# Stage A of sequences 4 to 7 as four 64x64 matmuls in the quadrants of the array

## The chip, the cores and the metric

The kernel runs on one core of one Trainium2 chip. The metric is the device time of one execution in microseconds (us), as the median of several runs. Each core has a matrix engine (PE, with its weight loads listed apart as PEld), a vector engine (DVE), a scalar engine (ACT), a general engine (POOL, which also issues DMAs) and a queue engine (SP, which issues most DMAs).

## The reference

Each of 8 sequences of 3008 rows and 256 channels is filtered in the frequency domain, and a gated feed-forward layer follows on the 24064 rows.

```python
X = np.fft.rfft(x, axis=1)                       # x: (8, 3008, 256)
Y = X * (filt_r + 1j * filt_i)[None, :, :]
y = np.fft.irfft(Y, n=3008, axis=1).reshape(24064, 256)
xn = y / np.sqrt(np.mean(y * y, axis=-1, keepdims=True) + 1e-06) * rms_g
g = xn @ w_gate                                  # d_ff = 1536
out = (g / (1 + np.exp(-g)) * (xn @ w_val)) @ w_out
```

## The kernel before

**The transform.** 3008 = 64 x 47, so the row index of a sequence is split into n2 (64 values) and n1 (47 values, padded to 48). Stage A transforms over n2 with one matmul for two n1 columns of 256 channels. Since n2 has 64 values and the array 128 rows, the x tile holds n1 = i in one half of its partitions and n1 = 24 + i in the other; the weights `wa` are block-diagonal, so that half of the 128x128 array multiplies zeros. In the kernel before the two halves alternate from partition to partition. Four x tiles of 6 n1 pairs make a sequence, and stage A has 12 units (`a_unit`, L201), each one matmul of 512 columns, and one copy out of PSUM by ACT or DVE. The result goes to DRAM (`z_store`, L209, a 384 KB DMA per x tile on SP's queue) and comes back with another axis on the partitions (`t2_load`, L219). Stage B (`b_unit`, L236) transforms over n1 and multiplies with the filter (`s_part`, L223, on DVE); its table is `wb`. The inverse stages follow (`bi_unit`, L280, `n_unit`, L306), then the norm on POOL, and transposes by DMA.

**The feed-forward layer.** 48 blocks (`b`, `m`) of up to 512 rows times 12 column groups `jt` make 576 items. An item is `gv` (L533: two matmuls for the gate, two for the value, 512 columns each, then a silu on ACT and a product on DVE) and, two items later, `down` (L554: four matmuls of 256 columns). The loop over the items, at the end of the kernel, is the frame into which all else is laid: the work of sequence b is put between the items of the sequences before it.

**The order.** It is written out by hand, and each engine works through its instructions in that order. A planner (`at`, `fit`, `a_plan`, `b_plan`, `norm_plan`) gives every unit an item as its slot; `fit` moves a unit later until its PSUM bank ("M" for pool psM, "B" for pool psB, each one bank) is free in that slot and ACT's and DVE's planned backlog stays under a bound. In `a_plan` (L764) the units of sequences 4 to 7 are asked for at slots `t - 87 + 4 * i`, where t is the first item of sequence b - 1; after each third unit a `z_store` follows one slot later, and the `x_load` (L174) of the same tile of the next sequence two slots later at the earliest. x tiles have 4 buffers, stage A's results (`t1`) have 3.

**The head.** Before the first item, sequence 0 is transformed in an order of its own (`a0_unit`, `f_unit`, `b_unit`, `yt0_unit` and others), while POOL issues the loads of x, the filter (`f_load`), the tables and the weights (`w_load`, L590) and writes negated filter columns (`f_neg`, L407) that `s_part` with e = 1 reads. Here too lie the only matmuls of the kernel whose operands are a few partitions high: the small transposes on L650 and L651, of one and two partitions, between matmuls on the full array.

**Names that the steps below touch.** `psa`: stage A's PSUM tile; `xc`: x tile; `pf`: output of the filler matmuls that `fill` (L423) issues in the head; `hh`, `po`: input and output of `down`; `pg`, `pv`: outputs of `gv`; `ws`, `fs`: staging tiles of weights and filter; `ff`: the filter as `s_part` reads it.

Of the kernel before, what the change touches and what calls it, by code (L numbers as in the profile page):

```python
# [17 lines left out]
N1 = 47  # L18
# [20 lines left out]
def _make_tables():  # L39
    n2 = np.arange(N2)  # L40
    wa = np.zeros((P, P))
    wai = np.zeros((P, P))
    for h in range(2):
        r = slice(h, P, 2)
        for k2 in range(K2):
            c = np.cos(2 * np.pi * ((n2 * k2) % N2) / N2)
            s = np.sin(2 * np.pi * ((n2 * k2) % N2) / N2)
            re = 4 * k2 + 2 * h
            wa[r, re] = c
            wai[re, r] = c * (1.0 if k2 == 0 else 2.0)  # L50
            if k2 == 0:
                alt = 1.0 - 2.0 * (n2 % 2)
                wa[r, re + 1] = alt
                wai[re + 1, r] = alt
            else:
                wa[r, re + 1] = -s
                wai[re + 1, r] = -2.0 * s
    n1 = np.arange(N1)
    rows = (n1 // H) * 2 * H + n1 % H
    re, im = rows, rows + H  # L60
    wb = np.zeros((P, K2, KR))
    wi0 = np.zeros((KR, KR))
    for k2 in range(K2):
        for q in range(SL):
            if q < H:
                k = k2 + 64 * q
                sign = 1.0
            else:
                j = q - H + 1
                k = 64 * j - (k2 if k2 else 32)  # L70
                sign = -1.0
                if j == H and k2:
                    continue
            th = 2 * np.pi * ((n1 * k) % N) / N
            c, sn = np.cos(th), np.sin(th)
            if k == 0 or k == NF - 1:
                sn = np.zeros(N1)
            if k2:
                wb[re, k2, q] = c
                wb[im, k2, q] = sign * sn  # L80
                wb[re, k2, SL + q] = -sn
                wb[im, k2, SL + q] = sign * c
            else:
                part = re if q < H else im
                wb[part, k2, q] = c
                wb[part, k2, SL + q] = -sn
                m = 1.0 if k in (0, NF - 1) else 2.0
                wi0[q, part] = m * c
                wi0[SL + q, part] = -m * sn
    f = np.float16  # L90
    r = np.arange(KR)
    wi = np.zeros((P, K2, KR))
    wi[:KR] = wb[:KR].transpose(2, 1, 0)
    wi[:KR, 0, :] = wi0
    wi[:, :, (r % H) * NR + r // H] = wi * S_INV_B
    tab = np.concatenate([wa.astype(f), (wai * S_INV_A).astype(f), np.eye(P).astype(f),
                          np.eye(P).astype(np.float32).view(f)], axis=1)
    return tab, wb.astype(f), wi.astype(f)


@with_exitstack
def kernel(
# [10 lines left out]
):  # L113
    nc = tc.nc

    tab_np, wb_np, wi_np = _make_tables()
    tab_d = nc.inline_tensor(tab_np, name="tab_t").ap()
    wb_d = nc.inline_tensor(wb_np, name="wb_t").ap()
    wi_d = nc.inline_tensor(wi_np, name="wi_t").ap()

    z_d = nc.dram_tensor("z_tmp", (B, K2, KR, D), FP16, kind="Internal").ap()

# [22 lines left out]
    idf = tab[:, 3 * P:5 * P].bitcast(FP32)  # L145
    wb = glob.tile([P, K2, KR], FP16)
    wi = glob.tile([P, K2, KR], FP16)
    uu = glob.tile([P, H, 2, P], FP16)
    left = glob.tile([P, 2, K2, 2], FP16)
    va = uu.rearrange("p c e t -> p (c e t)").rearrange("p (e k j) -> p e k j", e=2, k=K2)  # L150
# [16 lines left out]
    def raw(src, row, ap):  # L167
        return bass.AP(tensor=src.tensor, offset=src.offset + row * D, ap=ap)
# [5 lines left out]
    def x_load(b, c):  # L174
        t = xp.tile([P, XC, D], FP16, tag="xc", name="xc")
        row = b * N + c * XC
        src = lambda n, w, lo=0: raw(x.flatten_outer_dims(), row + lo, [[N1 * D, n], [H * D, 2], [1, w * D]])
        if b == B - 1 and c == NXC - 1:
            w = XC - 1
            nc.vector.memset(t[96:P, w, :], 0.0)  # L180
            nc.gpsimd.dma_start(t[:, 0:w, :].rearrange("p a d -> p (a d)"), src(N2, w))
            nc.gpsimd.dma_start(t[0:P - 2, w, :], src(N2 - 1, 1, w))
            nc.gpsimd.dma_start(t[P - 2:P - 1, w, :],
                                raw(x.flatten_outer_dims(), row + w + (N2 - 1) * N1, [[D, 1], [1, D]]))
        else:
            nc.gpsimd.dma_start(t.rearrange("p a d -> p (a d)"), src(N2, XC))  # L186
        st[b]["x"][c] = t
# [5 lines left out]
    def copy(eng, out, in_, scale=None):  # L193
# [4 lines left out]
        else:  # L198
            nc.vector.tensor_scalar(out=out, in0=in_, scalar1=scale, scalar2=None, op0=ALU.mult)

    def a_unit(b, i, eng="A", bk=0):  # L201
        c, r = divmod(i, XC // 2)
        if r == 0:
            st[b]["t1"][c] = t1p.tile([P, XC, D], FP16, tag="t1", name="t1")
        ps = bank(bk, "psa")
        nc.tensor.matmul(ps, wa, st[b]["x"][c][:, 2 * r:2 * r + 2, :], start=True, stop=True)  # L206
        copy(eng, st[b]["t1"][c][:, 2 * r:2 * r + 2, :], ps.rearrange("p (a d) -> p a d", a=2))

    def z_store(b, c):  # L209
        dst = z_d[b].rearrange("k (m i) d -> k m i d", m=NR)[:, :, c * XC:(c + 1) * XC, :]  # L210
        nc.sync.dma_start(dst, st[b]["t1"][c])

    def t2_tile(b, c):
        if b == 0 and c == 3:
# [65 lines left out]
    def bi_unit(b, i, eng="A", bk=0, ks=slice(0, 4)):  # L280
        g, dh = divmod(i, 2)
        yt = st[b]["yt"][g]
        ps = bank(bk, "psi")[:, 0:4 * KR].rearrange("p (k j) -> p k j", k=4)
        for k in range(4)[ks]:
            nc.tensor.matmul(ps[:, k, :], yt[0:KR, k, dh, :], wi[0:KR, 4 * g + k, :], start=True, stop=True)  # L285
        dst = uu[:, :, dh, 16 * g:16 * g + 16].rearrange("p c (k m) -> p c k m", k=4)
        copy(eng, dst[:, :, ks], ps.rearrange("p k (c m) -> p c k m", c=H)[:, :, ks])
        done[b] += ks.stop == 4
        if done[b] == K2 // 2:
            half = uu[:, H - 1, :, :].rearrange("p e (k m) -> p e k m", k=K2)  # L290
            if b % 2:
                nc.gpsimd.tensor_copy(out=half[:, :, :, 2:4], in_=left)
            else:
                nc.gpsimd.tensor_copy(out=left, in_=half[:, :, :, 0:2])

    def t4_load(b, c):
        t = t4p.tile([P, XC, D], FP16, tag="t4", name="t4")
# [312 lines left out]
    with tc.manual_schedule():  # L610
# [14 lines left out]
        nc.gpsimd.dma_start(wb[:, 16:K2, :], wb_d[:, 16:K2, :])  # L625
        nc.gpsimd.dma_start(wb[:, 0:4, :], wb_d[:, 0:4, :])
        nc.gpsimd.dma_start(wi, wi_d)
        w_load(0)
        w_load(1)
        nc.vector.memset(mhalf, -0.5)  # L630
# [133 lines left out]
        def a_plan(b, slots):  # L764
# [11 lines left out]
                        at(max(s + 2, XAT.get(b + 1, (0,) * 4)[i // 3]), x_load, b + 1, i // 3)  # L776
            return s + 1

        def b_plan(b, slots, lags, soft=()):
            for c in range(4):  # L780
                at(slots[0] - 4 + c if c < 3 else slots[4] + 1, t2_load, b, c)
            for i in range(16):
                if i in soft:
                    s0 = fit(slots[i], ("B", 0, 1), ("A", 0, 0.5))
                    at(s0, b_soft, b, i)
                else:
                    opts = [(k, ((k, 0, 1), (k, 1, 1), ("V", 0, 0.55), ("V", 1, 0.55)))
                            for k in ("BM" if b == 1 else "B")]
                    k, need = min(opts, key=lambda o: fit(slots[i], *o[1], keep=False))
                    s0 = fit(slots[i], *need)  # L790
                    at(s0, b_unit, b, i, 0 if k == "M" else 3)
                    at(s0 + 1, s_part, b, i, 1)
                    at(s0 + 2, add_unit, b, i)
                if i % 2:
                    at(s0 + 3 + (i in soft), yt_load, b, i // 2)
                    for u in (i - 1, i):
                        last = fit(s0 + lags[u % 2], ("M", 0, 1), ("A", 0, 0.49))
                        at(last, bi_unit, b, u)
            return last
# [10 lines left out]
        for b in range(1, B):  # L810
            t = (b - 1) * 72
            if b == 1:
                z = a_plan(b, [i for i in range(12)])
                b_at, lags = [z + 7 + 7 * i // 5 for i in range(16)], (9, 9)
                soft = range(2, 16, 4)
            elif b == 2:
                z = a_plan(b, [28 + 3 * i for i in range(12)])
                b_at, lags, soft = [z + 13 + 7 * i // 3 for i in range(16)], (8, 9), ()
            else:
                at_ = [72 + 3 * i if b == 3 else t - 87 + 4 * i for i in range(12)]  # L820
                z = a_plan(b, [s - (s % JT == 1) for s in at_])
                b_at, lags, soft = [t - (25 if b == 3 else 26) + 4 * i for i in range(16)], (8, 12), ()
            assert z + 3 <= b_at[0] - 4
            end = b_plan(b, b_at, lags, soft)
# [5 lines left out]
                norm_plan(b, m, (n_at + 8 * m, n_at + 8 * m + (4 if b > 1 else 2)), (2, 3, 7) if b > 1 else (2, 3, 6))  # L830

        for i, now in plan.items():
            if any(fn == a_unit and a[3] == 0 for fn, a in plan.get(i + 1, ())) and bi_unit in [fn for fn, _ in now]:
                now.sort(key=lambda u: u[0] == sq_unit)

        stores = {}
# [48 lines left out]
```

## Time and profile before

| what | value |
|---|---|
| median of 3 runs | 863.04 us (862.97 to 863.13) |
| span of the profiled execution | 861.4 us |
| PE busy in the span | 852.4 us (99%) |
| DVE, ACT, POOL busy | 557.2, 612.4, 297.8 us |
| TensorE clock granted, all 40 slices | 9 tenths or more |
| DMA, mean over the span | 125 GB/s |
| stage A matmuls on L206 | 84, from 38.5 to 605.1 us |
| of these, in sequences 4 to 7 | 48, from 234 to 612 us |

The span is the time from the first to the last instruction of the program in one execution under the hardware profiler; what the timed run has beyond it, 863.04 - 861.4 = 1.6 us, lies around it. In the lists of instructions a matmul's own duration includes the way through the array, so that consecutive ones overlap: the time from the start of one to the start of the next says what it costs. PEld rows are weight loads, which run beside the matmul before.

### The profile page before, as it was taken

The numbers are of one execution on the slowest core, as the hardware profiler recorded it, in microseconds if no ns is written. First come the engines' busy times: TensorE is split into PE (matmuls) and PEld (weight loads), VectorE is DVE, ScalarE is ACT, GpSimd is POOL, SyncE is SP. The second block draws the span as 40 slices with busy tenths as digits, with TensorE's granted clock in tenths as the row PEclk, the third lists the DMA queues.
The fourth block names the chain that finished last, engine by engine and source line by source line (L and its number), as shares of the span: only waits on it lengthen the run. The fifth ranks groups of instructions, "written<-read, shape, count | busy, mean of one in ns | idle before, by whom it ended". The sixth has DMA issues, their size and how long they took to land.

```text
span 861.4 us, 17024 instructions
## 1 busy us (share of the span) xinstructions
PE 852.4 (99%) x6142; PEld 532.2 (62%) x6142; DVE 557.2 (65%) x926; ACT 612.4 (71%) x1339; POOL 297.8 (35%) x346
## 2 busy tenths in 40 slices
PE   8999999999999999999999999999999999999997
PEld 6755666566666666666666666666666666665664
DVE  5857655776666666666666676767666665555554
ACT  4986777787588756887577856888567765777443
POOL 5725742453144322534034430444123430132000
PEclk9999999999999999999999999999999999999999
DMA  9995778765975476656755548433564331521101
GB/s 283 270 204 124 150 164 168 139 130 121 197 137 129 121 150 111 151 107 147 139 127 113 132 98 180 108 87 101 131 127 93 97 70 42 124 54 49 62 25 50
DMA packets 198237, 107.98 MB, mean 125 GB/s; under 512 B 158566, under 2 KB 182520, under 8 KB 198152
## 3 DMA queue, kind: packets, MB, share of 16 engines
q1 hardware_dynamic: 189464, 85.52, 44.1%
q0 software_dynamic: 8544, 21.24, 12.7%
q8 instruction: 48, 0.79, 0.4%
q14 instruction: 37, 0.30, 0.1%
q10 hardware_dynamic: 144, 0.13, 0.0%
HBM read 45.78 MB, written 35.65 MB: 95 GB/s over the span
## 4 chain that ended last, share of the span: by engine, by line
PE 96%; DMA 1%; ACT 1%; DVE 1%; issue 0%; POOL 0%; POOLq 0%
PE po L563 28%; PE pg L546 28%; PE pv L546 28%; PE psb L241 3%; PE psi L285 3%; PE psn L314 2%; PE psa L206 2%; DMA fs<-in_filt_i_dram 1%; PE psy L418 1%; PE psf L389 1%; PE pst L367 0%; ACT sg L550 0%; POOL xc L186 0%; DVE s L231 0%; DVE hh L551 0%
## 5 line engine op out<-in xcount | busy, mean ns | idle before, releaser
L551 DVE TENSOR_TENSOR hh<-pv,sg 128x512 f16<-128x512 f32 (+2 forms) x578 | 391.5, 678 | 286.4 <-ACT sg L550 221.9
L550 ACT ACTIVATE sg<-pg 128x512 f16<-128x512 f32 (+2 forms) x578 | 337.4, 584 | 217.6 <-PE pg L546 213.4
L546 PE MATMUL pg<-xn,wg 128*128 128x512 f16 (+2 forms) x1156 | 338.1, 374 | 0.1
L546 PE MATMUL pv<-xn,wv 128*128 128x512 f16 (+2 forms) x1156 | 338.1, 374 | 0.0
L563 PE MATMUL po<-wo,hh 128*128 128x256 f16 x2256 | 332.7, 273 | 0.0
L563 PEld LDWEIGHTS <-hh 128*128 128x128 f16 x2256 | 213.4, 98 | 105.5 <-issue 0.6
L268 POOL TENSOR_TENSOR ss<-s,s 128x384 f16<-128x384 f16 x112 | 101.9, 911 | 273.2 <-DVE s L234 245.2
L546 PEld LDWEIGHTS <-wv 128*128 128x128 f16 x1156 | 112.9, 98 | 130.7
L546 PEld LDWEIGHTS <-wg 128*128 128x128 f16 x1156 | 111.4, 98 | 17.0 <-issue 0.3
L340 POOL TENSOR_TENSOR xt<-y,rho 128x1024 f16<-128x1024 f32 (+1 forms) x46 | 85.4, 1856 | 2.8
L322 ACT ACTIVATE junk<-y 128x256 f16<-128x256 f32 x180 | 74.3, 413 | 2.8
L231 DVE TENSOR_TENSOR s<-psb,ff 128x384 f16<-128x384 f32 x124 | 67.6, 547 | 0.7 <-ACT ff L195 0.6
L234 DVE TENSOR_TENSOR s<-psb,ff 128x384 f16<-128x384 f32 x124 | 67.6, 546 | 0.0
L195 ACT ACTIVATE uu<-psi 128x384 f16<-128x384 f32 (+1 forms) x127 | 61.6, 486 | 1.5 <-DMA out_dram<-o 0.5
L195 ACT ACTIVATE y<-psn 128x512 f32<-128x512 f32 (+1 forms) x95 | 55.7, 588 | 4.2
L285 PEld LDWEIGHTS <-yt 96*128 96x128 f16 x512 | 35.4, 97 | 26.7 <-issue 1.0
L332 POOL TENSOR_TENSOR rho<-u,mhalf 128x4 f32<-128x4 f32 (+1 forms) x46 | 46.5, 1010 | 3.8
L330 POOL TENSOR_SCALAR u<-ss 128x4 f32<-128x4 f32 (+1 forms) x46 | 8.9, 193 | 104.8 <-ACT junk L322 103.8
L195 ACT ACTIVATE t<-psa 128x512 f16<-128x512 f32 x70 | 41.4, 594 | 3.1 <-PE psa L206 1.7
L285 PE MATMUL psi<-wi,yt 96*128 96x96 f16 x512 | 42.9, 205 | 0.1
L241 PE MATMUL psb<-wb,t 96*128 96x96 f16 x480 | 40.1, 206 | 0.3 <-DVE s L234 0.2
L241 PEld LDWEIGHTS <-t 96*128 96x128 f16 x480 | 28.7, 97 | 12.8 <-DVE s L234 3.3
(101 smaller groups left out, 366.2 us busy)
## 6 DMA issues: line engine op xcount, KB each, us to landing
out_dram<-o SPq DMA_DIRECT2D x40, 512.0 KB, 3.6
xc<-in_x_dram POOLq DMA_DIRECT2D x31, 384.0 KB, 5.6
z_tmp<-t SPq DMA_DIRECT2D x28, 384.0 KB, 2.7
t<-z_tmp SPq DMA_DIRECT2D x28, 384.0 KB, 6.0
out_dram<-o SPq DMA_DIRECT2D x7, 384.0 KB, 2.7
fs<-in_filt_i_dram POOLq DMA_DIRECT2D x3, 512.0 KB, 10.8
fs<-in_filt_r_dram POOLq DMA_DIRECT2D x3, 512.0 KB, 11.2
ws<-in_moe_w_gate_dram POOLq DMA_DIRECT2D x3, 512.0 KB, 9.8
```

The lines of the kernel that those rows point to most:

```text
L195: nc.scalar.activation(out=out, in_=in_, func=AXT.Copy, **({} if scale is None else {"scale": scale}))
L231: eng.tensor_tensor(out=o, in0=ps, in1=f1, op=ALU.mult)
L234: eng.tensor_tensor(out=o, in0=ps[:, :, ::-1, :], in1=f2, op=ALU.mult)
L241: nc.tensor.matmul(ps[:, ts(k, KR)], st[b]["t2"][kk // KC][:, kk % KC, ds(dh * P, P)], wb[0:KR, kk, :], start=True, stop=True)
L268: nc.gpsimd.tensor_tensor(out=ss3[g % 3][:, :, dh, 0:KR], in0=s[0], in1=s[1], op=ALU.add)
L285: nc.tensor.matmul(ps[:, k, :], yt[0:KR, k, dh, :], wi[0:KR, 4 * g + k, :], start=True, stop=True)
L322: nc.scalar.activation(out=junk, in_=y[:, i, ts(u, D)], func=AXT.Square, accum_out=ss[:, 2 * i + u:2 * i + u + 1])
L340: nc.gpsimd.tensor_tensor(out=xt[:, 0:n, :], in0=y.rearrange("p a (u d) -> p (a u) d", u=2)[:, 0:n, :], in1=rho[:, 0:n].unsqueeze(2).to_br ...
L546: nc.tensor.matmul(ps[:, 0:w], wt[:, dt_, ts(jt, P)], xn[:, q0:q1, dt_, :], start=(dt_ == 0), stop=(dt_ == 1))
L550: nc.scalar.activation(out=sg[:, c], in_=pg[:, 0:w], func=AXT.Silu)
L551: nc.vector.tensor_tensor(out=hh[:, c], in0=pv[:, 0:w], in1=sg[:, c], op=ALU.mult)
L563: nc.tensor.matmul(po[s4 // 2][:, s4 % 2, :], hh[:, ts(s4, P)], wo[:, jt, :], start=(jt == 0 and s4 % 2 == 0), stop=(jt == JT - 1 and (s4 ...
```

## The change

For sequences 4 to 7, `a_quad` takes the place of `a_unit`. It computes two units' worth at once: two x tiles (c = 0, 1) times two halves of their partitions (h = 0, 1) give four matmuls with K = 64 and 64 output columns of the array, each with 512 moving columns, with a place of its own among the four quadrants (`tile_position`). Input half h goes to PSUM bank h, tile c to the output partitions from 64 c. A sequence has 6 such quads, asked for at every second of the 12 slots, with banks M and B both and two copies, one by ACT and one by DVE. For the halves to lie in partitions 0 to 63 and 64 to 127, the x tiles of all sequences change their partition order, and the tables with them (`wa`, `wb`, `wi`, and the two columns of `uu` that `left` copies). The weights of a quadrant are a new 128x64 table `wq`, loaded on POOL's queue behind `wi`. Two `z_store`s are issued together after every third quad, and likewise the two `x_load`s of the next sequence. Sequences 1 to 3 keep `a_unit`.

```diff
+    wq = np.zeros((P, N2))
     for h in range(2):
-        r = slice(h, P, 2)
+        r = slice(h * N2, (h + 1) * N2)
+        o = slice(h, P, 2)
...
-            re = 4 * k2 + 2 * h
+            re = 4 * k2 + h
...
+            wq[r, 2 * k2:2 * k2 + 2] = wa[r, re:re + 4:2]
     n1 = np.arange(N1)
-    rows = (n1 // H) * 2 * H + n1 % H
-    re, im = rows, rows + H
+    re, im = n1, n1 + SL
...
-        src = lambda n, w, lo=0: raw(x.flatten_outer_dims(), row + lo, [[N1 * D, n], [H * D, 2], [1, w * D]])
+        src = lambda n, w, lo=0: raw(x.flatten_outer_dims(), row + lo, [[H * D, 2], [N1 * D, n], [1, w * D]])
...
+    QUAD = range(4, B)
+
...
+    def a_quad(b, i, bks=(0, 3), engs="AV"):
+        pr, j = divmod(i, XC // 2)
+        if j == 0:
+            st[b]["t1"][pr] = [t1p.tile([P, XC, D], FP16, tag="t1", name="t1") for _ in range(2)]
+        cols = slice(2 * j, 2 * j + 2)
+        pss = [bank(bk, "psa") for bk in bks]
+        for h in range(2):
+            for c in range(2):
+                r, o = slice(N2 * h, N2 * h + N2), slice(N2 * c, N2 * c + N2)
+                nc.tensor.matmul(pss[h][o, :], wq[r, :], st[b]["x"][2 * pr + c][r, cols, :],
+                                 start=True, stop=True, tile_position=(N2 * h, N2 * c))
+        for h in range(2):
+            copy(engs[h], st[b]["t1"][pr][h][:, cols, :], pss[h].rearrange("p (a d) -> p a d", a=2))
+
-    def z_store(b, c):
-        dst = z_d[b].rearrange("k (m i) d -> k m i d", m=NR)[:, :, c * XC:(c + 1) * XC, :]
-        nc.sync.dma_start(dst, st[b]["t1"][c])
+    def z_store(b, pr):
+        if b not in QUAD:
+            dst = z_d[b].rearrange("k (m i) d -> k m i d", m=NR)[:, :, pr * XC:(pr + 1) * XC, :]
+            nc.sync.dma_start(dst, st[b]["t1"][pr])
+            return
+        dst = z_d[b].rearrange("k (e h v c i) d -> h v c (k e) i d", h=2, e=2, v=2, c=2)
+        for h in range(2):
+            nc.sync.dma_start(dst[h, pr], st[b]["t1"][pr][h])
...
-                nc.gpsimd.tensor_copy(out=half[:, :, :, 2:4], in_=left)
+                nc.gpsimd.tensor_copy(out=half[:, :, :, 1:4:2], in_=left)
             else:
-                nc.gpsimd.tensor_copy(out=left, in_=half[:, :, :, 0:2])
+                nc.gpsimd.tensor_copy(out=left, in_=half[:, :, :, 0:4:2])
...
         nc.gpsimd.dma_start(wi, wi_d)
+        nc.gpsimd.dma_start(wq, wq_d)
         w_load(0)
         w_load(1)
...
+        def a_quad_plan(b, slots):
+            for i in range(6):
+                banks = (("M", 0, 1), ("B", 0, 1), ("B", 1, 1))
+                opts = [("AV", (*banks, ("A", 0, 0.6), ("V", 0, 0.68))),
+                        ("VA", (*banks, ("M", 1, 1), ("V", 0, 0.68), ("A", 1, 0.6)))]
+                e, need = min(opts, key=lambda o: fit(slots[2 * i], *o[1], keep=False))
+                s = fit(slots[2 * i], *need)
+                at(s, a_quad, b, i, (0, 3), e)
+                if i % 3 == 2:
+                    at(s + 1, z_store, b, i // 3)
+                    if b + 1 < B:
+                        for c in (2 * (i // 3), 2 * (i // 3) + 1):
+                            at(max(s + 2, XAT.get(b + 1, (0,) * 4)[c]), x_load, b + 1, c)
+            return s + 1
+
...
-                z = a_plan(b, [s - (s % JT == 1) for s in at_])
+                z = (a_quad_plan if b in QUAD else a_plan)(b, [s - (s % JT == 1) for s in at_])
```

More of the change, by code (lines that the diff above doesn't have):

```diff
@@ L47, in _make_tables @@
             s = np.sin(2 * np.pi * ((n2 * k2) % N2) / N2)
-            re = 4 * k2 + 2 * h
+            re = 4 * k2 + h
             wa[r, re] = c
-            wai[re, r] = c * (1.0 if k2 == 0 else 2.0)
+            wai[re, o] = c * (1.0 if k2 == 0 else 2.0)
             if k2 == 0:
                 alt = 1.0 - 2.0 * (n2 % 2)
-                wa[r, re + 1] = alt
-                wai[re + 1, r] = alt
-            else:
-                wa[r, re + 1] = -s
-                wai[re + 1, r] = -2.0 * s
+                wa[r, re + 2] = alt
+                wai[re + 2, o] = alt
+            else:
+                wa[r, re + 2] = -s
+                wai[re + 2, o] = -2.0 * s
+            wq[r, 2 * k2:2 * k2 + 2] = wa[r, re:re + 4:2]
     n1 = np.arange(N1)
-    rows = (n1 // H) * 2 * H + n1 % H
-    re, im = rows, rows + H
+    re, im = n1, n1 + SL
     wb = np.zeros((P, K2, KR))
@@ L97, in _make_tables @@
                           np.eye(P).astype(np.float32).view(f)], axis=1)
-    return tab, wb.astype(f), wi.astype(f)
+    return tab, wb.astype(f), wi.astype(f), wq.astype(f)
 @with_exitstack
@@ L114 @@
     nc = tc.nc
-    tab_np, wb_np, wi_np = _make_tables()
+    tab_np, wb_np, wi_np, wq_np = _make_tables()
     tab_d = nc.inline_tensor(tab_np, name="tab_t").ap()
@@ L119 @@
     wi_d = nc.inline_tensor(wi_np, name="wi_t").ap()
+    wq_d = nc.inline_tensor(wq_np, name="wq_t").ap()
     z_d = nc.dram_tensor("z_tmp", (B, K2, KR, D), FP16, kind="Internal").ap()
@@ L147 @@
     wi = glob.tile([P, K2, KR], FP16)
+    wq = glob.tile([P, N2], FP16)
     uu = glob.tile([P, H, 2, P], FP16)
@@ L181, in x_load @@
             nc.gpsimd.dma_start(t[:, 0:w, :].rearrange("p a d -> p (a d)"), src(N2, w))
-            nc.gpsimd.dma_start(t[0:P - 2, w, :], src(N2 - 1, 1, w))
-            nc.gpsimd.dma_start(t[P - 2:P - 1, w, :],
-                                raw(x.flatten_outer_dims(), row + w + (N2 - 1) * N1, [[D, 1], [1, D]]))
+            nc.gpsimd.dma_start(t[0:N2, w, :], raw(x.flatten_outer_dims(), row + w, [[N1 * D, N2], [1, D]]))
+            nc.gpsimd.dma_start(t[N2:P - 1, w, :],
+                                raw(x.flatten_outer_dims(), row + w + H, [[N1 * D, N2 - 1], [1, D]]))
         else:
@@ L832 @@
         for i, now in plan.items():
-            if any(fn == a_unit and a[3] == 0 for fn, a in plan.get(i + 1, ())) and bi_unit in [fn for fn, _ in now]:
+            if any(fn == a_quad or fn == a_unit and a[3] == 0 for fn, a in plan.get(i + 1, ())) and bi_unit in [fn for fn, _ in now]:
                 now.sort(key=lambda u: u[0] == sq_unit)
```

## The prediction

> **What bounds the kernel.** I read the engines' shares and the chain that ended last first.
>
> ```profile
> PE 852.4 (99%) x6142; PEld 532.2 (62%) x6142; DVE 557.2 (65%) x926; ACT 612.4 (71%) x1339; POOL 297.8 (35%) x346
> PE 96%; DMA 1%; ACT 1%; DVE 1%; issue 0%; POOL 0%; POOLq 0%
> ```
>
> PE is nearly the whole chain. Next the busy time by stretches where stage A of sequences 4 to 7 lies, and stage A's own share (all engines, then those instructions alone):
>
> ```profile
> 234.00:337.00 103.00, 103.00 (x722) 63.32 (x721) 67.12 (x111) 74.63 (x165) 36.32 (x41) 1.00 0.68 138
> ...
> 540.00:612.00 72.00, 72.00 (x519) 45.18 (x518) 50.30 (x86) 56.84 (x131) 30.47 (x31) 1.00 0.40 101
> 234.00:612.00 378.00, 18.21 (x48) 5.44 (x8) 23.72 (x40) 1.00 0.59 127
> ```
>
> Columns: time, then PE, PEld, DVE, ACT, POOL busy (last row: PE, DVE, ACT), granted clock, DMA share, GB/s. PE is never idle there and its clock is full, so each ns that PE saves or loses there is a ns of the kernel. What a matmul costs is seen between starts:
>
> ```profile
> 392.95 0.38 PE L546 MATMUL pv<-xn,wv 128*128 128x512 f16 x1
> 393.16 0.38 PE L206 MATMUL psa<-xc,tab 128*128 128x512 f16 x1
> 393.38 0.60 PE L563 MATMUL po<-wo,hh 128*128 128x256 f16 x4
> ```
>
> A stage A matmul lasts 0.38 us but holds the stream for 0.22; the trace's starts give 216 ns as the median, 109 for 256 columns, so 0.42 ns a column. Its weights are loaded while the matmul before runs.
>
> **The matmuls.** Two units, 2 x 216 = 432 ns, become four quadrant matmuls that, if they run side by side, hold PE for 216 ns plus what their starts lie apart. That saves at most 216 ns in each of 4 x 6 = 24 quads, 5.2 us. Against it stands the change of the array's division, in and out of every quad, since the neighbours use the full array. No 64x64 matmul is in this trace; the nearest rows are the transposes of one and two partitions in the head, between matmuls on the full array:
>
> ```profile
> 8.70 0.22 PE L357 MATMUL psa<-tab,xc 128*128 128x128 f16 x1
> 8.85 0.41 PE L650 MATMUL psg<-tab,tail 1*128 1x1 f32 x4
> 9.12 0.20 PE L651 MATMUL psg<-tab,tail 2*128 2x2 f32 x1
> ...
> 8.64 0.10 PEld L357 LDWEIGHTS <-xc 128*128 128x128 f16 x1
> 8.85 0.32 PEld L650 LDWEIGHTS psg<-tab,tail 1*128 1x128 f32 x4
> 9.09 0.14 PEld L651 LDWEIGHTS psg<-tab,tail 2*128 2x128 f32 x1
> 9.24 0.11 PEld L426 LDWEIGHTS <-ss 128*128 128x128 f16 x2
> ```
>
> Everywhere else a weight load begins as the matmul before it begins; here it waits. From the last L357 start to the first L650 are 151 ns where that matmul takes 55: 96 lost. It is not the change of type: L367 (f16) to L389 (f32), both on the full array, is 56 ns, nothing lost. The next start follows after 85 ns, the later ones after 61 to 63: 24 for a weight load that nothing covers. On the way out L426 starts 129 ns after L651: 68 over 61; the start after that comes at 225 instead of 216: 9. In and out together 96 + 24 + 68 + 9 = 197 ns. The exit could be dearer: of the pitch of 61, some 53 are the load of 128 columns at 0.42 ns, so that L651 itself holds PE for 8 only; then the 129 contain 121 instead of 68, and the switch is 250.
>
> Between the four starts lie the next weight loads:
>
> ```profile
> L206 PEld LDWEIGHTS <-tab 128*128 128x128 f16 x84 | 8.2, 98 | 8.2
> L418 PEld LDWEIGHTS <-s 128*96 128x96 f16 x128 | 8.2, 123 | 1.3 <-DVE s L231 1.0 <-DVE s L234 0.2
> ```
>
> 96 columns take longer than 128, so narrow weights don't get the quick load; at one column per 0.42 ns 64 of them take 27 ns (my estimate). Bounds: 0 (all start at once) and 62 (the pitch on L650). I take 27, three times: 81. A quad is then 197 + 81 + 216 = 494 ns against 432: **62 ns dearer, 24 x 62 = +1.5 us.** Bounds: 62 - 81 = -19 ns, -0.5 us; 62 + 105 + 53 = 220 ns, +5.3 us.
>
> **The copies.** Two per quad as before, but DVE's go from 8 to 24 (16 x 0.68 = +10.9 us) and ACT's from 40 to 24. In those 378 us DVE is about two thirds busy, and the product of `gv` is needed only two items later: nothing; without that cover it is the fourth rival. **z_store and x_load**: as many DMAs of 384 KB as before, now in pairs, so on SP's queue the second store (0.35 us to issue) and on POOL's the second load (0.64) come before the transposes and adds behind them. The data of sequence 4's first quad is needed earlier, both tiles at once: the second is issued at 224.87 and lands after 5.4 us, at 230.3, and stage A begins at 234.4. Nothing. The stores end four slots sooner, so `t2_load` has more room. The strided `left` copies are 7 of 288 ns on POOL, which is 35% busy: nothing, at most 2 us if each doubled with no cover.
>
> **The load of `wq`.** It is small, but stands in POOL's queue in the head, where everything is late already:
>
> ```profile
> 14.46 0.53 POOL L627 DMA_DIRECT2D wi<-wi_t  x1 [0.74 <-DMA fs<-in_filt_r_dram]
> 15.74 0.74 POOL L594 DMA_DIRECT2D ws<-in_moe_w_gate_dram  x1 [0.75 <-DMA fs<-in_filt_i_dram]
> 17.03 0.72 POOL L594 DMA_DIRECT2D ws<-in_moe_w_val_dram  x1 [0.55 <-DMA fs<-in_filt_r_dram]
> 18.59 0.70 POOL L594 DMA_DIRECT2D ws<-in_moe_w_gate_dram  x1 [0.83 <-PE pst L367]
> 19.28 0.72 POOL L594 DMA_DIRECT2D ws<-in_moe_w_val_dram  x1
> 20.28 0.84 POOL L409 TENSOR_SCALAR ff<-ff 128x192 f32<-128x192 f32 x2 [0.27 <-ACT ff L195]
> ...
> 21.20 1.47 DVE L234 TENSOR_TENSOR s<-psb,ff 128x384 f16<-128x384 f32 x3
> 23.31 2.10 DVE L231 TENSOR_TENSOR s<-psb,ff 128x384 f16<-128x384 f32 x4 [0.64 <-ACT ff L195]
> ```
>
> From the ninth to the sixteenth each issue comes 0.28 us after the landing of the eighth before it. One more issue moves each later one back by a place: `wq` goes at 15.74, and the fourth `ws` waits for the last `fs`, issued at 10.07, landed at 21.24. It is issued at 21.52 instead of 19.28, `f_neg` behind it starts at 22.26 instead of 20.28, and the first DVE product that reads its 0.35 us result at 22.6 instead of 21.20. Three products of 1.47 us end at 24.07; the next began at 23.31. **+0.8 us**, and from 25 to 37 us DVE has no gap that could take it back. Bounds: 0 (the limit is not of eight) and 1.4 (the 0.64 us of idle time don't help).
>
> **Sum.** 861.4 + 1.5 + 0.8 = 863.7 for the span; 1.6 lie around it: **865.3 us, +0.27%.** Its own range: 863.0 - 0.5 = 862.5 to 863.0 + 5.3 + 1.4 = 869.7.
>
> **The rivals.** A measurement here tells 0.2% from no change, that is 861.3 to 864.8.
>
> *All four start together.* Starts 0 apart: -19 ns a quad, -0.5 + 0.8 = **863.3 us**, no change. For it: nothing obliges the four loads to queue, their quadrants being apart. Against: loads on L650 queue. The Trainium skill's TensorE: Matmul & The Clock Gate (Measured speedup vs the span model) puts packed matmuls about 4 ns apart; by that a quad would be 425 ns and the time 863.6. No run here shows it yet.
>
> *Switching costs little or nothing in a running stream*; this one ends on the faster side. 216 + 81 - 432 = -135 ns, 24 times -3.2 us, + 0.8: **860.6 us.** It decides once entry and exit together stay under 135 ns, where I have 197. For it: my row is of other tiles (one partition, f32), seen once. Against: both its ends show the loss. The Trainium skill's TensorEngine Tiling (Array Packing), Key Properties, says that any change of mode drains the engine; this row agrees, with 96 ns.
>
> *Neighbours on the same rows take turns.* If the second weight load of a row half waits until the matmul on these rows has ended, then in the order of the code three passes follow one another: 3 x 216 + 2 x 27 = 702 instead of 297, +467 ns a quad, +11.2 + 0.8: **875.0 us.** Against it: today each load starts 1 to 2 ns after a matmul that uses the same rows. The Trainium skill's TensorE: Matmul & The Clock Gate (The mechanism) states such a wait for packed matmuls; no row here has two of them.
>
> *The banks come late.* A quad needs M and B free at once and loads DVE more; if DVE's products on B (546 ns) run late, PE waits in each quad. The 16 waits over 60 ns after 70 us have a mean of 145 ns: 24 x 145 = 3.5 on top, **868.8 us.** Against: from 234 to 612 us PE hardly waits at all now. It decides only if DVE is behind in most quads.
>
> *The quadrants run one after the other*, and the change doesn't do what it says: 4 x 216 + 197 = 1061 ns, +629, 24 times +15.1, + 0.8: **878.9 us.** Nothing in this trace excludes it.
>
> **How the numbers follow.** Forecast 0.40 (slower 0.31, same 0.09); starting together 0.15 (same 0.13, faster 0.02); cheap switching 0.24 (faster 0.19, same 0.05); late banks 0.09, taking turns 0.08, one after the other 0.04, all slower. Together faster 0.21, same 0.27, slower 0.52. The predicted time is the likeliest case's, 865.3. From 859.6 to 869.7 the range holds the forecast's bounds and most of the cheap switching (its floor, starts 0 apart, is 858.6); outside are some 0.06 below and 0.12 above.
>
> **What would show it.** Right: the four starts on `psa` some 27 ns apart; the full-array load before and after each quad later by about 100 ns than it would be; some 494 ns from a quad's predecessor's end to the matmul behind it; in the head the fourth `ws` issued near 21.5 and the L231 products from about 24.1. Wrong: no hole at a quad's edges (cheap switching), starts on `psa` 216 apart (turns, or one after the other), holes that end with DVE (banks), or the fourth `ws` still near 19.3.

## The result and the profile after

The changed kernel takes **1120.88 us** (1118.17 to 1122.16, 4 runs) against 863.09 us: **1.298 times as long (95% interval 1.296 to 1.300)**, where 865.3 us were forecast. From the page of the changed kernel: busy time, the granted clock in 40 slices, the queue of POOL's DMAs, the chain.

```profile
PE 900.8 (80%) x6190; PEld 546.6 (49%) x6190; DVE 568.0 (51%) x942; ACT 604.1 (54%) x1323; POOL 305.6 (27%) x347
PEclk7988988988976979899597997969989999999999
q0 software_dynamic: 37136, 21.37, 11.5%
PE 66%; DMA 26%; POOL 2%; SPq 2%; issue 2%; ACT 1%; DVE 1%; POOLq 0%; DVEq 0%
```

PE has 48 matmuls more and is busy for 48 us longer, but it is idle for a fifth of the span, and DMAs make up a quarter of the chain where they had 1%. The changed kernel's busy time by stretches (PE, PEld, DVE, ACT, POOL, clock, DMA share, GB/s):

```profile
45.00:234.00 189.00, 147.64 (x1063) 89.95 (x1061) 93.11 (x163) 110.63 (x246) 65.56 (x77) 0.88 0.83 112
337.00:435.00 98.00, 68.49 (x418) 38.52 (x418) 39.83 (x65) 44.46 (x102) 26.08 (x27) 0.81 1.03 81
861.00:1119.00 258.00, 246.50 (x1624) 151.43 (x1624) 148.17 (x232) 158.06 (x336) 52.70 (x55) 0.98 0.31 75
```

From 45 to 234 us PE is idle for 41 us already, and no quad runs before 331 us. By then the items of the feed-forward layer start 97 us later than before, so this part of the loss cannot be the quads'. The last long wait ends at 868 us; from 880 us to the end the delay stays at 258 us. What PE waits for is named by the changed kernel's list of waits (total, times, longest, in us):

```profile
PEld L310 <- DMA yt<-ss: 146.2, 12, 22.9
...
PEld L212 <- DMA xc<-in_x_dram: 19.4, 2, 11.8
```

The list of the kernel before has no wait of PE for `yt`, and the transposition `yt_load` is not touched by the change. Three rows on the x tiles show what became slow: the landing times of `xc` (minimum, median, maximum) before and after, and the queue's packets before.

```profile
DMA to landing us min/median/max: 4.0/5.5/10.2
```
```profile
DMA to landing us min/median/max: 18.4/22.8/34.4
```
```profile
q0 software_dynamic: 8544, 21.24, 12.7%
```

The same bytes take four times as long, and the queue has 28592 packets more. They carry no x data: both traces have 3968 packets of 3072 bytes, 248 ns each as the median, but 4-byte packets, called fillers here, went from 946 to 29537. The pattern explains the count. The source of an x load began with a dimension of 64 (`[[N1 * D, 64], [H * D, 2], ...]`) and now begins with one of 2 (`[[H * D, 2], [N1 * D, 64], ...]`). If a load's 128 packets then lie on 2 of the 16 DMA engines, 64 on each, and each of the other 14 gets a filler for every one, that makes 32 loads x 14 x 64 = 28672, 80 more than counted (the last tile's small loads have a new pattern too); and 64 x 248 ns = 15.9 us a load, against a fastest landing of 18.4. The trace names no engine, but its packets have times, and these agree. The load issued at 128.72 us has its 128 packets from 130.30 to 147.14, and for 15.3 of these 16.8 us exactly two are under way. In the kernel before, the load issued at 224.87 has up to 20 at a time and is through in 3.9 us. The quads' stores have the same form (`dst[h, pr]` begins with c, of 2): on SP's queue the page counts 189464 packets before and 189240 after, 224 fewer, which is 16 stores x 14.

The Trainium skill's DMA: Bandwidth & Descriptors (Why a DMA increments its semaphore by 16 and not by 1) says just this: the number of engines is the largest up to 16 that divides the slowest dimension of both patterns, so a first dimension of 2 gives two engines. This case's counts agree.

One such wait in the changed kernel, from the lists in order of time of POOL, SP and PE (start, duration, what, idle time before and its end):

```profile
128.72 0.88 POOL L190 DMA_DIRECT2D xc<-in_x_dram  x1 [0.23 <-issue]
...
130.58 13.90 SPq L300 DMA_TRANSPOSE yt<-ss  x2
...
138.56 0.59 PE L571 MATMUL pv<-xn,wv 128*128 128x512 f16 x2
149.30 0.50 PE L310 MATMUL psi<-wi,yt 96*128 96x96 f16 x4 [10.14 <-DMA yt<-ss]
149.92 1.05 PE L571 MATMUL pg<-xn,wg 128*128 128x512 f16 x2
```

The x load is issued at 128.72 and lands 18.8 us later, at 147.5. The transposition issued 2 us behind it does not get through beside it: from 136 to 147 us SP's queue moves 44 to 76 packets of 256 bytes in each us, and 350 in the next, when the load is over. PE is out of work at 139 and starts again at 149.3. Then two 512-column matmuls last 1.05 us together where they lasted 0.59: at 427 ns from start to start PE runs at half its pitch, with a granted clock of 0.50, until 152.3 us. In the whole trace 20 waits of over 1.5 us make 214 us, and matmuls at half pitch take some 43 us more than at full pitch (1.6 before): together nearly all of the 258 us.

### The profile page after: what moved, and what is told of

The parts are those of the page before. It is cut to its first block, busy times and chain, and to the rows that moved or that the text cites. A ratio compares the mean times of both kernels' runs of the same rounds, so it can differ in the third digit from the quotient of the medians.

```text
span 1119.7 us, 17115 instructions
## 1 busy us (share of the span) xinstructions
PE 900.8 (80%) x6190; PEld 546.6 (49%) x6190; DVE 568.0 (51%) x942; ACT 604.1 (54%) x1323; POOL 305.6 (27%) x347
## 3 DMA queue, kind: packets, MB, share of 16 engines
q1 hardware_dynamic: 189240, 85.52, 55.0%
## 4 chain that ended last, share of the span: by engine, by line
PE 66%; DMA 26%; POOL 2%; SPq 2%; issue 2%; ACT 1%; DVE 1%; POOLq 0%; DVEq 0%
PE po L588 20%; PE pg L571 19%; PE pv L571 18%; DMA yt<-ss 15%; DMA xc<-in_x_dram 6%; DMA t<-uu 2%; PE psi L310 2%; PE psb L266 2%; PE psn L339 2%; DMA z_tmp<-t 2%; DMA t<-z_tmp 1%; POOL ss L293 1%; PE psa L224 1%; SPq L324 1%; ACT sg L575 1%
## 5 line engine op out<-in xcount | busy, mean ns | idle before, releaser
L571 PE MATMUL pg<-xn,wg 128*128 128x512 f16 (+2 forms) x1156 | 350.2, 385 | 0.1
L571 PE MATMUL pv<-xn,wv 128*128 128x512 f16 (+2 forms) x1156 | 348.4, 384 | 0.0
L588 PE MATMUL po<-wo,hh 128*128 128x256 f16 x2256 | 348.0, 281 | 0.0
L588 PEld LDWEIGHTS <-hh 128*128 128x128 f16 x2256 | 218.6, 101 | 114.6 <-issue 16.1
L571 PEld LDWEIGHTS <-wv 128*128 128x128 f16 x1156 | 115.7, 100 | 138.9 <-issue 14.6
L310 PE MATMUL psi<-wi,yt 96*128 96x96 f16 x512 | 45.7, 214 | 140.4 <-DMA yt<-ss 140.3
L571 PEld LDWEIGHTS <-wg 128*128 128x128 f16 x1156 | 114.8, 101 | 20.1 <-issue 0.3
L199 ACT ACTIVATE y<-psn 128x512 f32<-128x512 f32 (+1 forms) x95 | 55.7, 588 | 18.4 <-PE psn L339 14.3
L199 ACT ACTIVATE t<-psa 128x512 f16<-128x512 f32 x54 | 31.8, 592 | 42.4 <-PE psa L212 22.5
L339 PE MATMUL psn<-t,tab 128*128 128x512 f16 x92 | 35.7, 388 | 11.1 <-DMA t<-uu 11.0
## 6 DMA issues: line engine op xcount, KB each, us to landing
xc<-in_x_dram POOLq DMA_DIRECT2D x31, 384.0 KB, 22.7
```

Of the source, the lines that this page charges most:

```text
L199: nc.scalar.activation(out=out, in_=in_, func=AXT.Copy, **({} if scale is None else {"scale": scale}))
L571: nc.tensor.matmul(ps[:, 0:w], wt[:, dt_, ts(jt, P)], xn[:, q0:q1, dt_, :], start=(dt_ == 0), stop=(dt_ == 1))
L588: nc.tensor.matmul(po[s4 // 2][:, s4 % 2, :], hh[:, ts(s4, P)], wo[:, jt, :], start=(jt == 0 and s4 % 2 == 0), stop=(jt == JT - 1 and (s4 ...
```

## The experiments

The theory, *two engines*: a DMA that begins with a dimension of 2 lies on two DMA engines, and what needs these waits. The rival, *divided array*: the quads, their switches and the low clock after them. The first four kernels ran together.

**e1_no_quads**: no sequence uses quads.

```diff
-    QUAD = range(4, B)
+    QUAD = range(B, B)
```

> The changed kernel without quads: all sequences use the 128x128 matmul, so there is no divided array and no store on two rows of 64; only the new partition order of the x tiles, its loads and the load of wq are left. Theory 'two engines' (a DMA whose access pattern begins with a dimension of 2 is carried by 2 of the 16 DMA engines, and whatever else needs these two waits): 28 x loads after the head stay slow, time 1000 to 1110 us, x loads land after 18 us or more. Rival 'divided array' (the quads, their switches and the lower clock after them are the loss): 863 to 866 us.

One run: **1076.4 us**. The divided array is not there, and five sixths of the loss are: 1076.4 - 863.3 = 213 of 258 us. The granted clock is low here too, 0.91 as the mean.

**e2_x_halves**: each x load in two, of 64 partitions and a first dimension of 64.

```diff
-        src = lambda n, w, lo=0: raw(x.flatten_outer_dims(), row + lo, [[H * D, 2], [N1 * D, n], [1, w * D]])
+        half = lambda h, w: raw(x.flatten_outer_dims(), row + h * H, [[N1 * D, N2], [1, w * D]])
...
-            nc.gpsimd.dma_start(t.rearrange("p a d -> p (a d)"), src(N2, XC))
+            for h in range(2):
+                nc.gpsimd.dma_start(t[N2 * h:N2 * h + N2].rearrange("p a d -> p (a d)"), half(h, XC))
```

> The changed kernel with each x load issued as two loads of 64 partitions, whose first dimension is 64; the quads' stores stay as they are. 'Two engines': what is left are 16 stores of 64 x 124 ns = 8 us on each of two engines, 880 to 960 us; x loads land after 5 to 8 us. 'Divided array': nothing changes, 1100 us or more.

One run: **964.5 us**, just above the range. x loads land after 7.0 us as the median. What is left is the stores, and they cost more than expected. The packets say why. The two stores of a pair are issued 0.6 us apart; in the five pairs whose packets stand alone, two are under way for most of 17 to 21 us and never more than four. So both stores lie on the same two engines and hold them for 256 x 124 / 2 ns = 15.9 us, where the expectation had 8.

**e3_z_halves**: the quads' stores in halves, the x loads as in the change.

```diff
-            nc.sync.dma_start(dst[h, pr], st[b]["t1"][pr][h])
+            for c in range(2):
+                nc.sync.dma_start(dst[h, pr, c], st[b]["t1"][pr][h][N2 * c:N2 * c + N2])
```

> The changed kernel with each store of a quad issued as two of 64 partitions; the x loads stay as they are. 'Two engines': the x loads keep most of the loss, 1000 to 1110 us. 'Divided array': 1100 us or more, like the changed kernel.

One run: **1081.7 us**, inside the range: the x loads keep most of the loss.

**e4_both_halves**: both edits.

> Both kinds of DMA in halves of 64 partitions; the quads as in the change. 'Two engines': the loss is gone, and what is left is what the quads and the head cost: 863 to 870 us (quads at +14 ns each as the changed kernel's starts show it, 0.3 us, up to 1.5 us; the head later by 0.8 us for wq and by up to 3 us for the four more issues on POOL's queue). 'Divided array': 1050 us or more.

Five runs: **870.0 us, 1.0083 (1.0069 to 1.0097)**. Of its page, the clock and the software queue:

```profile
PEclk9999999999999999999999999999999999999999
...
q0 software_dynamic: 8976, 21.26, 12.2%
```

The clock is full again and the fillers are gone, with all quads in place. The rival has fallen: the low clock comes with the waits, without quads (e1_no_quads) too, and goes with them. From 870.0, the x loads alone add 1081.7 - 870.0 = 212 us, the stores alone 964.5 - 870.0 = 94, and both 251: less than the sum, presumably since they partly delay the same transpositions. Each single run stands far outside the 4 us by which repeated ones differ at most.

In these runs the first dimension and the size of a DMA changed together. **e13_x_columns** keeps e3_z_halves' stores and cuts the x loads along the columns: half the size, but 128 partitions and a first dimension of 2.

```diff
-            nc.gpsimd.dma_start(t.rearrange("p a d -> p (a d)"), src(N2, XC))
+            for a in (0, XC // 2):
+                nc.gpsimd.dma_start(t[:, a:a + XC // 2, :].rearrange("p a d -> p (a d)"), src(N2, XC // 2, a))
```

> The quads' stores in halves, and each x load as two loads of half the size as well, but cut along the columns: each has all 128 partitions and still begins with the dimension of 2. 'Two engines' (the first dimension decides): the x loads stay slow, as with one load per tile (1081.7 us), 1040 to 1110 us. Rival 'size of a DMA' (two smaller loads in place of one are what cured it): 868 to 875 us, as with the halves of 64 partitions.

One run: **993.0 us**, 47 below the range, 123 above the halves. Its landing times of `xc`:

```profile
DMA to landing us min/median/max: 10.8/15.7/26.8
```

57809 packets of 4 bytes: twice as many loads, each with its 14 x 64 fillers, so each is still on two engines, and a pair of half loads that stands alone has four packets under way most often. A half-size load occupies them for 64 x 135 ns = 8.6 us instead of 15.9 and so should hold up a transposition for less; that was missing in the expectation. The slowest landing of `yt` agrees, 16.4 us where e3_z_halves has 23.3. The first dimension decides whether a DMA is confined, its size for how long. That is shown for the x loads; for the stores it rests on the packets' counts and times.

**What is left of e4_both_halves**, 6.8 us, is taken apart in the next four, which ran together (before: 863.12).

**e5_layout_alone**: x loads in halves, no quads.

> Like the kernel with both kinds of DMA in halves, but without quads: all sequences use the 128x128 matmul. Theory 'quads cost the rest': 864.4 to 865.4 us, the 1.6 us that the head was later, so that the quads' part of the other kernel's 870.0 is some 5 us. Rival 'the added DMA issues cost the rest': 869 to 870 us.

**865.1 us, 1.0028 (1.0018 to 1.0039).** The quads with their stores cost 870.0 - 865.1 = 4.9 us, the head 2.0. Whole x loads cost 1076.4 - 865.1 = 211 us without quads, as much as with them. In the trace the delay stands at 1.6 to 1.7 us from the head to the end.

**e6_mixed_order**: sequences 0 to 3 keep the old order and whole loads, all else as in e4_both_halves.

```diff
         o = slice(h, P, 2)
+        ri = o
...
-            wa[r, re] = c
+            wa[ri, re] = c
...
+            if b not in QUAD:
+                nc.gpsimd.dma_start(t.rearrange("p a d -> p (a d)"),
+                                    raw(x.flatten_outer_dims(), row, [[N1 * D, N2], [H * D, 2], [1, XC * D]]))
```

> Sequences 0 to 3 keep the old partition order and one load per x tile; sequences 4 to 7 have the new order, loads and stores in halves, and the quads; wq is loaded behind wi on POOL's queue as in the change. The head then has only the load of wq more than before: by the prediction's step +0.8 us, with the quads' 5.4 us 869.0 to 869.8 us. If wq costs nothing, 868.3 to 868.8 us.

**870.3 us, 1.0083 (1.0069 to 1.0097)**, above the range: no gain over e4_both_halves.

**e7_wq_elsewhere**: the same, with `wq` on SP's queue.

```diff
         nc.sync.dma_start(tab, tab_d)
+        nc.sync.dma_start(wq, wq_d)
...
-        nc.gpsimd.dma_start(wq, wq_d)
```

> The same with wq loaded on SP's queue behind tab, so that POOL's queue in the head is that of the kernel before: 0.7 to 0.9 us less than with wq behind wi if that step holds (about 868.5 us), no difference if it doesn't.

**869.3 us, 1.0074 (1.0062 to 1.0087)**: 1.0 us less, but the intervals of the two overlap. In the traces the fourth `ws` is issued at 19.77 instead of 21.58, and the delay behind the head is 0.5 instead of 2.0 us; but the profiled execution of e6_mixed_order also had a granted clock of 0.83 from 20 to 30 us, where this one had 1.00, so that difference is not the load's alone. The next tests the step by itself.

**e8_before_plus_load**: the kernel before and one more small load.

```diff
         nc.gpsimd.dma_start(wi, wi_d)
+        nc.gpsimd.dma_start(wq, wq_d)
```

> The kernel before with nothing but a load of 16 KB behind wi on POOL's queue (the first 64 columns of the table; nobody reads it). By the prediction's step +0.8 us: 864.0 to 864.2 us, with the fourth load of ws issued near 21.5 us. Rival (the limit isn't of eight, or the delay is taken back): 863.1 to 863.5 us.

**864.25 us, 1.0016 (1.0008 to 1.0025).** POOL's and DVE's lists in order of time:

```profile
21.42 0.72 POOL L596 DMA_DIRECT2D ws<-in_moe_w_val_dram  x1 [1.50 <-DMA fs<-in_filt_r_dram]
22.26 1.47 POOL L411 TENSOR_SCALAR ff<-ff 128x192 f32<-128x192 f32 x3
...
22.66 1.50 DVE L236 TENSOR_TENSOR s<-psb,ff 128x384 f16<-128x384 f32 x3 [1.50 <-POOL ff L411]
```

The fourth `ws` at 21.42 (forecast 21.52), `f_neg` at 22.26 (22.26), DVE's product at 22.66 (22.6), and behind the head every item of the trace is 0.8 us later.

**The quads.** In the traces of the kernels with halves many quads' third matmul starts late. From e4_both_halves, PE and DVE in order of time:

```profile
355.16 0.40 PE L226 MATMUL psa<-xc,wq 64*64 64x512 f16 x2
355.94 0.40 PE L226 MATMUL psa<-xc,wq 64*64 64x512 f16 x2 [0.37 <-DVE s L262]
...
354.86 0.56 DVE L579 TENSOR_TENSOR hh<-pv,sg 128x384 f16<-128x384 f32 x1 [0.67 <-ACT sg L578]
355.34 0.55 DVE L262 TENSOR_TENSOR s<-psb,ff 128x384 f16<-128x384 f32 x1
```

The second pair writes bank B, which stage B's second product still reads until 355.89; that product stands on DVE behind `hh`. In e7_wq_elsewhere such waits make 3.7 us. Four kernels on top of it, run together (before: 863.19):

**e9_after_down**: a quad comes behind the item's `down`.

```diff
-            todo = (late if fn == q_unit else plan).setdefault(slot, [])
+            todo = (late if fn in (q_unit, a_quad) else plan).setdefault(slot, [])
```

> The kernel with mixed order and wq on SP's queue (869.3 us), with each quad issued behind the item's down instead of before it, 0.4 us later in PE's stream. Theory 'late bank': the third matmul of a quad waits for bank B, which DVE's second product of stage B still reads; these waits (3.7 us between the second and third start of quads in the trace of that kernel) shrink to under 1 us: 865.4 to 866.5 us. Rival 'the wait moves' (DVE's copies and the next item's work come late instead): 868.5 us or more.

**865.9 us, 1.0034 (1.0022 to 1.0047)**, 3.5 us less, and the waits shrink to 0.8 us, three quads of sequence 5. The late bank is shown. One of the 21 other quads, PE and its weight loads in order of time:

```profile
456.82 0.49 PE L596 MATMUL po<-wo,hh 128*128 128x256 f16 x3
457.24 0.41 PE L231 MATMUL psa<-xc,wq 64*64 64x512 f16 x4
457.58 0.61 PE L579 MATMUL pg<-xn,wg 128*128 128x512 f16 x2
...
457.24 0.11 PEld L231 LDWEIGHTS <-wq 64*64 64x64 f16 x4 [0.21 <-issue]
457.58 0.11 PEld L579 LDWEIGHTS <-wg 128*128 128x128 f16 x2 [0.23 <-issue]
```

The four start within 10 ns (3, 3, 4). By the starts in the trace the entry loses 93 to 94 ns, the next full-array matmul starts 332 ns after the fourth, 116 more than 216, and the one after that 11 late: 93 + 10 + 332 + 11 = **446 ns against 432, +14 ns a quad**.

**e10_quads_twice**: each quad's four matmuls issued twice.

```diff
-        for h in range(2):
+        for h in (0, 1, 0, 1):
             for c in range(2):
```

> The same kernel (869.3 us) with the four matmuls of each quad issued twice, into the same banks. If entering and leaving the divided array is paid once per quad and what runs within it only streams, the second four cost 216 ns: 24 x 0.22 = +5.2 us, 874 to 875 us. If each pass of four pays the drain or the quadrants don't run side by side, +8 us and more: 877 us or more.

**873.35 us, 1.0117 (1.0103 to 1.0131)**: 4.0 us more than e7_wq_elsewhere, somewhat less than expected. By the starts in the trace the second four begin 240 ns behind the first, but the full-array matmul behind them starts 308 ns after the last instead of 332, so they add 216 ns a quad, 5.2 us, as expected; the waits for bank B are the same as without them. The two waits of some 1 us for a transposition shrink from 2.0 to 1.0 us together, which makes the difference. The second four run side by side, and the switch is paid once per entry, not per matmul.

**e11_stores_apart**: the second half of a pair's stores three items later.

```diff
-                    at(s + 1, z_store, b, i // 3)
+                    at(s + 1, z_store, b, i // 3, (0,))
+                    at(s + 4, z_store, b, i // 3, (1,))
```

> The same kernel (869.3 us) with the second half of a pair's stores three items later, so that two instead of four stores stand together on SP's queue. In that kernel's trace PE waits twice for some 1.0 us for a transposition that stood behind four stores and two output stores: 867.0 to 867.8 us. Rival (the queue is late for another reason): 869 us.

**868.9 us, 1.0066 (1.0052 to 1.0080)**, above the range and not to be told from 869.3. In its trace one of the two waits of 1 us is gone and the other, 0.9 us, has stayed.

**e12_both**: e9_after_down and e11_stores_apart together.

> Quads behind down and stores apart, together: if both waits go, what is left above the kernel before is 24 x 14 ns = 0.3 us for the quads themselves and 0.5 us in the head: 863.6 to 865.0 us. If one of the waits only moves: 866 us or more.

**865.5 us, 1.0025 (1.0016 to 1.0035)**, above the range and still slower than the kernel before. In its trace the delay is 1.6 us: 0.3 for the quads, 0.8 for bank B in sequence 5, some 0.5 for the transpositions' queue. No version with quads beat the kernel before.

## Why the prediction was wrong

**The step that failed** is "z_store and x_load: as many DMAs of 384 KB as before ... Nothing." It counted issues, bytes and queues, and took a landing of 5.4 us over from a load of another pattern. The new partition order put the dimension of 2 in front in both DMAs. That cost some 251 us (1120.9 - 870.0), the x loads alone 212; no rival contained it, and the range ended at 869.7. The diff shows the exchanged dimensions, and the time of a packet lay in the trace of before: 64 of 248 ns one after the other on an engine are 15.9 us, where 8 were 2.0. That a first dimension of 2 leaves two engines no row of that trace shows; the runs here do.

**The path**: that PE sets the time and each ns it waits counts was right, and made the loss so large: PE's waits and its half pitch after them are nearly the whole of it.

**The matmuls**: the mechanism held, with other sizes. Switching was put at 197 ns and measures 93 + 116 + 11 = 220; the starts were put at 81 ns and measure 10. The estimate of 27 ns for each further weight load fell: loads for different quadrants do not queue. A quad costs +14 ns instead of +62, 0.3 us instead of 1.5. The rival "all four start together" was right about the starts. The Trainium skill's TensorE: Matmul & The Clock Gate (Measured speedup vs the span model) puts them about 4 ns apart; the traces agree, with 3 to 4. "Cheap switching", "taking turns" and "one after the other" are refuted by the entry of 93 ns and the starts. A wait for the same rows, on which "taking turns" rested, does not occur here: the second matmul, on the rows of the first, starts 3 ns behind it.

**The copies** were put at nothing; the fourth rival, late banks, priced 3.5 us for it, and the waits for bank B make 3.7. That the sums agree is partly luck: the rival had 145 ns in each of 24 quads, and the trace has 0.1 to 0.8 us in ten of them. It was given a chance of 0.09. DVE's two thirds of busy time were the wrong evidence: the question was what stands before the product on its queue, at this place.

**The load of wq** was right: forecast +0.8 us, in the trace 0.8, by the times +1.1 (0.7 to 2.2).

**Sum without the failed step**: 870.0 us measured in e4_both_halves, where 865.3 was forecast and 869.7 the upper end. Its span is 6.9 us over that of before: in the trace 1.6 in the head (0.8 forecast; the halves' own issues, which the change didn't have, come on top), 0.3 for the quads (1.5 forecast), 3.7 for the banks and 1.3 for two waits for a transposition (both at nothing).

## What to carry to other kernels

When a layout changes, write out the access pattern of each DMA and look at its first dimension, not only at bytes, packets and issues: confined to two engines, the same load landed four times later and held up transpositions that had nothing to do with it. Four quadrant matmuls do run side by side, but in a stream of full-array matmuls each entry and exit took 220 ns, as much as the 216 ns that two 512-column matmuls turned into one could save. It should pay with more work per entry, since a second four cost 216 ns where they would replace 432; no run here has a kernel that uses them.

## What the runs showed of the hardware

After long waits PE's matmuls start at half the pitch (213 to 214 ns instead of 109 for 256 columns): for 3.0 us behind a wait of 10.1 us that ended at 149.3, for 4.4 us behind one of 22.4 that ended at 554.2. Over the changed kernel's run this costs some 43 us. Loads confined to two engines run beside each other: the four x loads at the start, issued from 1.2 to 3.9 us, landed at 19.6, 20.9, 22.7 and 22.9, each after 18 to 20 us, with eight packets under way most often: four loads, two engines each, and not the same two. The paired stores of SP's queue did share theirs (e2_x_halves). Unused engines of a DMA from POOL's queue got 4-byte packets of 9 ns; those of a DMA from SP's queue got none.
